# Reordering the first 45 microseconds of a fused attention and channel-mix kernel: the odd rows, mu, the norm products and the copy of v of block 1

## The chip, the cores and the metric

The kernel runs on one core of one Trainium2 chip. The metric is device time in microseconds (us) of that core. A kernel's time is the median of several executions, and most executions agree within 0.3%. The span that the trace shows is about 1.9 us shorter than the measured time of the same execution (510.4 against 512.35 us for the kernel before). All experiments ran beside executions of the kernel before on the same chip, and ratios are taken within such a call.

## The reference, cut to what matters

```python
# q, k, v: (4, 6208, 256) float32; x: (4, 6208, 256); d_ff = 1024
qn = q / (norm(q, axis=1) + 1e-6)             # column norms over all 6208 rows
kn = k / (norm(k, axis=1) + 1e-6)
s  = kn.transpose(0, 2, 1) @ qn / tau         # one 256 x 256 matrix per batch
a  = softmax(s, axis=-1)
x  = v @ a                                    # the attention's output

x_prev = x shifted by one row
xk = mu_k * x + (1 - mu_k) * x_prev           # xr the same with mu_r
out = sigmoid(xr @ w_r) * (relu(xk @ w_k) ** 2 @ w_v)
```

The first product with v needs the softmax of batch 0, and that needs *all* 6208 rows of q and k of batch 0. So nothing of the second half can start before 12.7 MB have been loaded. The work on batch 1 to 3 is then woven into the second half.

## The kernel before

The rows of q and k of batch 0 arrive in groups of 512, two smaller groups last. The 64 rows that are left over ("odd rows", group 0) are spread over a full tile that is cleared first. For every group VectorE (DVE) and ScalarE (ACT) cast to bf16 and square k, and TensorE (PE) adds to the covariances.

```python
def group_load(b, g):
    ...
            f = pq.tile([P, S, C], F32, ...)
            if g == 0:
                nc.vector.memset(f, 0.0)
                (nc.scalar, nc.gpsimd)[i].dma_start(f[0:P:P // (L // S)], qk_src(t, b, g))
            else:
                nc.sync.dma_start(f[:rows, :n], qk_src(t, b, g))
...
for g in order(0):                       # groups 1, 2, 0, 3, ... ; LAST is the last
    ...
    group_cast(g, pending)
    cov_first(g)                         # covariances of the group, on PE
    if g == DIRECT:                      # the last but two
        keep_warm(2)                     # two matmuls whose result nobody reads
        norms_first(DIRECT - 1)          # column sums of k squared, on PE
    if g > DIRECT:
        norms_first(g - 1)
    if g == NB - 1:
        v_load(0)
norms_first(LAST)
```

Then comes the chain from the last rows to the first block: the diagonals of q's covariance (DVE), two square roots (ACT), the table load for Exp (ACT), the scaling, four transposes (PE), Exp (ACT), the shares `a_sb` (DVE), the first products `x` (PE). PE takes its instructions in order. The loads of v and of the weights are issued from GpSimd (POOL) and cast to bf16 on the way. The v of blocks 0 to 3 is transposed on PE; from block 4 on a DMA transposes it.

```python
v_load(1)
nc.gpsimd.dma_start(w_k_sb, ...)
...
diagonals()
root(0)
root(1)
nc.scalar.activation(gate, ones[:, 0:1], AF.Exp)     # brings the table load forward
...
exp()
go = v_transpose_pe(1, nc.scalar.copy)   # 8 transposes on PE now; go() is the copy out, later
keep_warm(3)
weigh_first(0); weigh_first(1)           # a_sb
difference(1)
for a in range(2):
    for ih in range(2):
        product(a, ih)                   # the first x
    for dh in range(2):
        mix_first("xk", a, dh)
go()                                     # v of block 1 leaves PSUM here, on ACT
```

## Time and profile before

The kernel before takes 512.03 us (median of 3, 511.83 to 512.68). First the head of its page: the span, the busy time of each engine with its share of the span, and the busy tenths in 40 equal slices.

```profile
span 510.4 us, 9358 instructions
PE 484.9 (95%) x3450; PEld 331.0 (65%) x3450; DVE 447.1 (88%) x756; ACT 446.8 (88%) x927; POOL 101.7 (20%) x149
...
PE   3667999999999999999999999999999999999997
...
PEclk9999999999999999999999999999999999999999
```

PE is the full engine from the fifth slice on (one slice is 12.8 us), but for two waits of 1.2 us in all near 132 us. Its table of windows says the same with numbers. The first two figures of a line are the window and its length.

```profile
core 0: us, PE busy (x) PEld busy (x) DVE busy (x) ACT busy (x) POOL busy (x), PEclk, DMA share, GB/s
54.00:90.00 36.00, 35.88 (x257) 24.27 (x256) 33.47 (x52) 35.90 (x82) 11.00 (x19) 1.00 1.22 208
90.00:130.00 40.00, 40.00 (x294) 28.03 (x291) 39.27 (x59) 39.87 (x91) 10.69 (x16) 1.00 1.32 166
```

So a start of the stream one microsecond earlier is worth about one microsecond, and only the first 54 us can give it. The yardstick below is the first `vr` matmul, the first of the down-projection: from there PE is full. These are the lines of that head, from the timeline of the kernel before (start in us, duration, engine, line, operation, out<-in, count; in brackets the idle time just before it and what ended it):

```profile
start us, us, engine line op out<-in xcount [idle before <-releaser]
35.77 0.43 DVE L147 CAST qk<-f 128x512 bf16<-128x512 f32 x1
...
38.30 0.49 DVE L266 TENSOR_TENSOR dg<-s_ps,ident_f 128x128 f32<-128x128 f32 x2 [2.10 <-PE s_ps L183]
...
41.41 0.61 PE L359 MATMUL vT_ps<-ident,v_bf 128*128 128x128 bf16 x8
41.61 0.47 ACT L309 ACTIVATE e_sb<-st_ps,rn 128x256 f32<-128x256 f32 x1 [0.56 <-PE st_ps L301]
...
42.92 0.39 PE L404 MATMUL x_ps<-vT,a_sb 128*128 128x256 bf16 x2 [0.25 <-DVE a_sb L322]
...
45.22 1.03 ACT L365 COPY vT<-vT_ps 128x1024 bf16<-128x1024 bf16 x1
...
46.30 0.67 PE L428 MATMUL kT_ps<-xk,w_k_sb 128*128 128x256 bf16 x4 [0.66 <-ACT vT L365]
...
53.13 0.59 PE L380 MATMUL xT_ps<-vT,a_sb 128*128 128x512 bf16 x2 [0.22 <-DVE vT L365]
...
53.99 0.38 PE L521 MATMUL vr_ps<-w_r_sb,xr 128*128 128x256 bf16 x2
```

Read it so: the last rows of k land at 35.75 us, and their cast starts at 35.77; the diagonals (`dg`) start at 38.30, behind PE's covariances; Exp (`e_sb`) at 41.61. The first x product waits for the shares `a_sb`. The copy at 45.22 keeps PE waiting for 0.66 us. The first product of block 2 (L380) waits 0.22 us for its v.

### The profile page before, as it was taken

The page shows a single profiled execution, that of the slowest core. Times are in us where ns is not written, and L with a number is a line of the kernel's source. Part 1 is how long each engine was busy: PE and PEld are TensorE (multiplying, and loading weights), DVE is VectorE, ACT ScalarE, POOL GpSimd, SP SyncE. Part 2 cuts the span into 40 slices and gives each one's busy share as a digit, 9 for nine tenths or more (in the row PEclk, how much of TensorE's full clock was granted, in tenths as well). Part 3 has the DMA queues.
Part 4 walks back from the last instruction along what each step waited for, and adds up shares of the span by engine and source line. Part 5 has one row for each costly group of instructions (what it writes and reads, how often), then busy time and mean ns, then how long its engine had stood idle before and what let it go on. Part 6 is the DMA issues. An engine that isn't in the chain of part 4 may idle for free. (4 is left out here: it accounts for less than half of the span.)

```text
span 510.4 us, 9358 instructions
## 1 busy us (share of the span) xinstructions
PE 484.9 (95%) x3450; PEld 331.0 (65%) x3450; DVE 447.1 (88%) x756; ACT 446.8 (88%) x927; POOL 101.7 (20%) x149
## 2 busy tenths in 40 slices
PE   3667999999999999999999999999999999999997
PEld 1334666776566667667666677667666666666666
DVE  4867899999999999999979999999878787878884
ACT  4867999999899999999899999999897888878884
POOL 2044341223054132121243133000131100000000
PEclk9999999999999999999999999999999999999999
DMA  8999999999989999997599999924397653423123
GB/s 303 410 327 194 196 198 219 158 162 202 154 161 197 182 207 172 172 179 139 95 158 158 219 180 191 181 67 125 82 169 146 141 108 89 101 77 91 41 84 104
DMA packets 133423, 83.46 MB, mean 164 GB/s; under 512 B 50717, under 2 KB 126689, under 8 KB 133377
## 3 DMA queue, kind: packets, MB, share of 16 engines
q0 software_dynamic: 56688, 33.07, 50.1%
q1 hardware_dynamic: 76496, 49.59, 41.1%
q8 instruction: 27, 0.44, 0.4%
q10 hardware_dynamic: 192, 0.20, 0.1%
q14 instruction: 20, 0.16, 0.1%
HBM read 78.71 MB, written 25.43 MB: 204 GB/s over the span
## 5 line engine op out<-in xcount | busy, mean ns | idle before, releaser
L493 ACT ACTIVATE kr<-kT_ps 128x512 bf16<-128x512 f32 (+1 forms) x389 | 231.5, 607 | 28.0 <-PE kT_ps L488 24.1
L525 PE MATMUL vr_ps<-w_v_sb,kk 128*128 128x256 bf16 x1536 | 231.1, 273 | 0.2
L488 PE MATMUL kT_ps<-xk,w_k_sb 128*128 128x512 bf16 (+1 forms) x778 | 229.4, 377 | 0.1
L525 PEld LDWEIGHTS <-kk 128*128 128x128 bf16 x1536 | 149.5, 98 | 59.1 <-DVE kk L506 1.3
L535 DVE SCALAR_TENSOR_TENSOR res<-res,vr_ps 128x256 f32<-128x256 f32 x192 | 79.8, 416 | 42.6 <-ACT res L534 42.6
L506 DVE TENSOR_TENSOR kk<-kr 128x1536 bf16<-128x1536 bf16 (+2 forms) x148 | 116.9, 790 | 0.2 <-ACT kr L493 0.2
L488 PEld LDWEIGHTS <-w_k_sb 128*128 128x128 bf16 x778 | 75.3, 98 | 27.6 <-issue 0.6
L224 DVE TENSOR_TENSOR acc<-acc,sq 128x1024 f32<-128x1024 f32 x69 | 84.0, 1217 | 0.0
L534 ACT ACTIVATE res<-vr_ps 128x256 f32<-128x256 f32 x192 | 76.4, 398 | 1.3 <-PE vr_ps L525 1.3
L521 PE MATMUL vr_ps<-w_r_sb,xr 128*128 128x256 bf16 x384 | 73.3, 272 | 1.2 <-DVE res L535 1.2
L473 DVE SCALAR_TENSOR_TENSOR xk<-delta,mu_t,xT 128x512 bf16<-128x512 bf16 x94 | 70.0, 745 | 0.0
L473 DVE SCALAR_TENSOR_TENSOR xr<-delta,mu_t,xT 128x512 bf16<-128x512 bf16 x94 | 69.9, 744 | 0.0
L521 PEld LDWEIGHTS <-xr 128*128 128x128 bf16 x384 | 37.6, 98 | 46.4 <-issue 2.7
L382 ACT CAST xT<-xT_ps 128x512 bf16<-128x512 f32 x94 | 55.3, 588 | 12.2 <-PE xT_ps L380 12.1
L380 PE MATMUL xT_ps<-vT,a_sb 128*128 128x512 bf16 x188 | 55.9, 379 | 0.5 <-ACT xT L382 0.2
L236 PE MATMUL s_ps<-qk 128*128 128x256 bf16 (+1 forms) x294 | 55.8, 273 | 0.0
L130 POOL DMA_DIRECT2D qk<-in_q_dram x39 | 26.4, 676 | 143.1 <-ACT kr L493 61.1
L220 ACT ACTIVATE sq<-qk 128x1024 f32<-128x1024 bf16 (+1 forms) x49 | 51.0, 1040 | 0.0
L343 POOL DMA_DIRECT2D v_bf<-in_v_dram x48 | 36.8, 769 | 47.3 <-DMA vT<-v_bf 22.3
L183 PE MATMUL s_ps<-qk 128*128 128x384 bf16 (+1 forms) x104 | 20.2, 338 | 15.3 <-ACT qk L145 13.9
L463 DVE TENSOR_TENSOR delta<-xT 128x1024 bf16<-128x1024 bf16 x47 | 32.2, 686 | 1.8 <-ACT xT L382 1.8
L236 PEld LDWEIGHTS <-qk 128*128 128x128 bf16 (+1 forms) x294 | 28.5, 98 | 5.6 <-issue 0.8
(106 smaller groups left out, 249.2 us busy)
## 6 DMA issues: line engine op xcount, KB each, us to landing
out_dram<-res SPq DMA_DIRECT2D x47, 512.0 KB, 4.1
v_bf<-in_v_dram POOLq DMA_DIRECT2D x48, 256.0 KB, 9.2
qk<-in_q_dram POOLq DMA_DIRECT2D x36, 256.0 KB, 7.9
qk<-in_k_dram POOLq DMA_DIRECT2D x36, 256.0 KB, 8.8
f<-in_q_dram SPq DMA_DIRECT2D x11, 512.0 KB, 10.1
f<-in_k_dram SPq DMA_DIRECT2D x11, 512.0 KB, 10.2
vT<-v_bf SPq DMA_TRANSPOSE x44, 6.9
f<-in_q_dram SPq DMA_DIRECT2D x2, 256.0 KB, 9.0
```

Source lines behind the costliest of these rows:

```text
L224: nc.vector.tensor_tensor(sums[b], sums[b], t, op=OP.add)
L236: nc.tensor.matmul(s_ps[:, ih, :], rows_at(qk, b, g, 0)[:rows, s, ih * P:(ih + 1) * P], rows_at(qk, b, g, 1)[:rows, s, :], start=t0 and ih ...
L380: nc.tensor.matmul(xT_ps, a_sb[:, b, ih, dh * P:(dh + 1) * P], vT[:, :, ih, :], start=ih == 0, stop=ih == 1)
L382: nc.scalar.copy(xT[:, dh, 1:], xT_ps)
L473: nc.vector.scalar_tensor_tensor(o[:, dh], st[i, "d"][:, dh], mu[:, dh:dh + 1], st[i, "x"][:, dh, :M], op0=OP.mult, op1=OP.add)
L488: nc.tensor.matmul(kT_ps[:, :m], w_k_sb[:, dh, fh * P:(fh + 1) * P], xk[:, dh, :m], start=dh == 0, stop=dh == 1)
L493: nc.scalar.activation(kr, kT_ps[:, :m], AF.Relu, scale=0.5 ** 0.5)
L506: nc.vector.tensor_tensor(st[i, "kk"][:, fh // 4 * 4 + lo:fh + 1, :m], kr, kr, op=OP.mult)
L521: nc.tensor.matmul(vr_ps[:, D:], xr[:, dh, s * P:(s + 1) * P], w_r_sb[:, dh, :], start=dh == 0, stop=dh == 1)
L525: nc.tensor.matmul(vr_ps[:, :D], kk[:, fh, s * P:(s + 1) * P], w_v_sb[:, fh, :], start=fh == 0, stop=fh == 7)
L534: nc.scalar.activation(res[:, s], vr_ps[:, D:], AF.Tanh, scale=0.5)
L535: nc.vector.scalar_tensor_tensor(res[:, s], res[:, s], 1.0, vr_ps[:, :D], op0=OP.add, op1=OP.mult)
```

## The change

Its intent is to shorten that head. (1) The odd rows become one row per partition, 64 partitions, on ScalarE's queue ahead of everything, so that no tile has to be cleared and the work on them is small; mu is loaded last, behind the last group. (2) All norm products go behind the last covariances, two warming matmuls there go (and one of the three after the transposes of v of block 1), and the diagonals are issued between the last covariances. (3) The transpose and copies of mu move into the chain. (4) The copy of v of block 1 is made before x of block 0 instead of after it, and v of block 2 is transposed one slot later.

```diff
     def sizes(b):
-        return [S] * NB + [S // 2] * 2 if b == 0 else [1] + [S] * NB
+        return [1] + [S] * (NB - 1) + [S // 2] * 2 if b == 0 else [1] + [S] * NB
 ...
-                if g == 0:
-                    nc.vector.memset(f, 0.0)
-                    (nc.scalar, nc.gpsimd)[i].dma_start(f[0:P:P // (L // S)], qk_src(t, b, g))
-                else:
-                    nc.sync.dma_start(f[:rows, :n], qk_src(t, b, g))
+                (nc.sync if g else nc.scalar).dma_start(f[:rows, :n], qk_src(t, b, g))
 ...
     def cov_first(g, diagonal=None):
 ...                                   # after the last group's diagonal blocks:
+            diagonal()
 ...
-    nc.gpsimd.dma_start(mu_rows[0:2], moe_mu_k...)      # at the very start
-    nc.gpsimd.dma_start(mu_rows[2:4], moe_mu_r...)
 ...
+        if g == LAST:
+            nc.sync.dma_start(mu_rows[0:2], moe_mu_k...)
+            nc.sync.dma_start(mu_rows[2:4], moe_mu_r...)
         group_cast(g, pending)
 ...
-        cov_first(g)
-        if g == DIRECT:
-            keep_warm(2)
-            norms_first(DIRECT - 1)
-        if g > DIRECT:
-            norms_first(g - 1)
+        cov_first(g, diagonals)
 ...
-    norms_first(LAST)
+    norms_first()                      # all of them
 ...
-    diagonals()
     root(0)
     root(1)
 ...
+    mu_ps = ...; nc.tensor.transpose(mu_ps, mu_rows, ident_f[:4, :4])
     turn()
     invert_first(1)
     go()
+    nc.vector.tensor_copy(mu_t, mu_ps)
+    nc.vector.tensor_scalar_add(less, mu_t, -1.0)
     difference(0)
     exp()
-    go = v_transpose_pe(1, nc.scalar.copy)
-    keep_warm(3)
+    v_transpose_pe(1, nc.scalar.copy)()
+    keep_warm(2)
 ...
-    go()
 ...
-            if (i, j) in ((-1, 5), (0, 4)):
+            if (i, j) in ((-1, 6), (0, 4)):
                 v_transpose_pe(i + 3, nc.vector.tensor_copy)()
```

Left out: the sum of k's squares is split in two around k's cast, the copy of the second half of x is one instruction instead of two, and the third up-projection of block 0 is whole instead of in halves.

## The prediction

> **What bounds the kernel now.** From about 54 us on it is TensorE: the table of windows has PE busy 40.0 of 40 us in most stretches, and the trace shows two PE gaps over 60 ns after 54 us (0.82 and 0.35 us, near 132 us). So only the first 54 us count: when that stream starts.
>
> - Loads, 2 to 35.75 us. From 16 to 33 us the stream runs at its ceiling (about 410 GB/s, one 512 KB load per 1.28 us). 12.7 MB at that rate take 31.0 us; first packet 1.79 us, last landing 35.75 us (DMA issues and packets). About 2.5 us are lost early: 233 to 370 GB/s between 4 and 10 us, with single 4 KB packets of 0.9 to 1.6 us instead of 0.16. The Trainium skill ("DMA: Bandwidth & Descriptors", why a DMA increments by 16) says a DMA is done when all its engines are; here the rate falls from 34 us while the slowest finish.
> - Chain after the last load: DVE cast ends 36.20, but PE reaches the last cov group only at 37.55 (cov, two warming matmuls, norm products queue); the diagonal products start on DVE at 38.30, behind the last cov matmuls; Exp 41.61; first x product 42.92.
> - First block: ACT is full from 45 to 50 us, with the 1.03 us copy of v of block 1 (45.22) in front of kr; PE waits 0.66 us.
>
> **What changes, with costs**
> 1. Odd rows: the full-tile work of group 0 (casts 0.69+1.03, square 1.05, three adds 1.1 us, two 0.91 us memsets) shrinks to 64x256 pieces. ACT is behind only until 20 us, so by itself this is worth nothing. But no Pool-queue transfer (k rows, mu) runs inside the stream any more. If the stall at 4 to 6 us came from those, the stream ends earlier: I count 1.2 us (0 to 2.3).
> 2. Norms behind the last cov, warming matmuls out, second half of the k sums behind the k cast: PE starts the last group at 36.35 instead of 37.55. Diagonals are issued before the remaining four cov matmuls: DVE starts at 36.7 instead of 38.30. Those matmuls probably then wait for DVE's reads of the same banks, 0.3 us; norms (0.8 us in one run) finish by 38.5, the table load (1.28) by 40. Exp at 40.2 to 40.3: 1.4 us earlier.
> 3. mu copies move into DVE's chain (+0.35 us), which had nearly that slack: first x product about 1.3 us earlier.
> 4. v of block 1 copied in ACT's 1.18 us idle: xT of block 1 comes about 1.8 us earlier in all. But v of block 2 now goes behind a 0.6 us square on DVE, so the first product of block 2 (now 53.13) gains only 1.2 to 1.3.
>
> Sum: 1.25 (steps 2 to 4) + 1.2 (step 1) = 2.45 us, carried to the end by a saturated PE.
>
> **Predicted: 509.6 us, 80% range 507.7 to 511.2.** Faster by over 2%: 0.01; within 2%: 0.985; slower: 0.005.
>
> **What would show it.** Landing of the last k rows at about 34.5 (step 1); diagonals starting about 0.9 us after that landing, against 2.55 now (step 2); no ACT v copy between xT and kr (step 4); first vr matmul (now 53.99) at about 51.5.
>
> **What would make it wrong.** The early DMA stall has another cause and stays (about 510.8); 1 KB packets of the odd rows delay the head of the stream; PE turns cold without warming matmuls (the Trainium skill, "TensorE: Matmul & The Clock Gate", Part 1: idle windows halve the clock; here the first group takes 0.32 us per matmul, later ones 0.16); v or w landing late.

## More of the kernel before

The eight transposes of v of block 1 (L359) start at 41.41 and wait for nothing: that v had landed at 39.29, 2.1 us earlier.

The landing of v of block 0 and of block 1 is in the source view of the line that loads v, for the two issues at 33.3 and 34.1 us:

```profile
DMA to landing us min/median/max: 4.8/5.0/5.2
```

## The result, and the profile after

The changed kernel took 511.32 us (median of 4, 511.01 to 512.12) against 512.36 us for the kernel before (median of 4, 511.83 to 513.21). The ratio is 0.9981, with a 95% interval from 0.9962 to 0.9999. Here and below a ratio is the mean time of one kernel's fast runs over the mean of the other's in the same rounds, so it is not quite the ratio of the medians. That is within 2%, as predicted, but 1.7 us above the predicted time and above the range's upper end of 511.2.

From the page of the changed kernel:

```profile
span 510.2 us, 9336 instructions
...
PEclk9998999999999999999999999999999999999999
```

The fourth digit of the clock row is new: in the slice from 38 to 51 us PE did not have its full clock all the time. The timeline of the changed kernel shows what is there. The lines answer to those shown of the kernel before, with two more (L190 and L591).

```profile
34.84 0.43 DVE L149 CAST qk<-f 128x512 bf16<-128x512 f32 x1
...
35.49 0.49 DVE L272 TENSOR_TENSOR dg<-s_ps,ident_f 128x128 f32<-128x128 f32 x2 [0.23 <-PE s_ps L184]
35.84 0.69 PE L190 MATMUL s_ps<-qk 128*128 128x256 bf16 x4 [0.33 <-DVE dg L272]
...
39.11 0.46 ACT L315 ACTIVATE e_sb<-st_ps,rn 128x256 f32<-128x256 f32 x1
...
40.39 1.04 PE L365 MATMUL vT_ps<-ident,v_bf 128*128 128x128 bf16 x8 [1.50 <-DMA v_bf<-in_v_dram]
41.22 1.06 PE L591 MATMUL junk_ps<-fill,ones 128*128 128x512 bf16 x2
41.47 1.01 ACT L371 COPY vT<-vT_ps 128x1024 bf16<-128x1024 bf16 x1 [1.35 <-PE vT_ps L365]
42.08 0.63 PE L410 MATMUL x_ps<-vT,a_sb 128*128 128x256 bf16 x2
...
52.94 0.59 PE L386 MATMUL xT_ps<-vT,a_sb 128*128 128x512 bf16 x2 [0.83 <-DVE vT L371]
...
53.80 0.38 PE L527 MATMUL vr_ps<-w_r_sb,xr 128*128 128x256 bf16 x2
```

Everything up to Exp is where the prediction wanted it, or better: the last k rows land at 34.82 instead of 35.75, the diagonals start 0.67 us after that landing, Exp starts 2.5 us earlier. Then the line at 40.39 takes it back. The transposes of v of block 1 are now asked for at 38.89, but that v lands at 40.35. PE stands for 1.50 us, and the x products, which need none of it, are queued behind. The same eight transposes and the products then run slowly (1.04 us instead of 0.61, and 0.63 instead of 0.39 for two products): PE has half its clock, as the windows show.

```profile
core 0: us, PE busy (x) PEld busy (x) DVE busy (x) ACT busy (x) POOL busy (x), PEclk, DMA share, GB/s
36.00:38.00 2.00, 1.95 (x34) 1.74 (x32) 1.57 (x6) 0.67 (x3) 2.00 (x4) 1.00 1.06 107
...
40.00:42.00 2.00, 1.61 (x10) 1.14 (x11) 1.01 (x4) 0.65 (x3) 0.55 (x1) 0.50 1.12 209
42.00:44.00 2.00, 2.00 (x14) 1.53 (x13) 0.12 (x1) 1.01 (x3) 0.54 (x1) 0.71 1.16 203
```

The clock records put it at 0.5 from 39.76 to 43.18 us, 3.41 us long. And v of block 1, issued at 33.26 us, 0.8 us earlier than in the kernel before, took 7.1 us to land instead of 5.2 (source view of the line that loads v, for the same two issues; block 1 is the longer of the two):

```profile
DMA to landing us min/median/max: 5.1/6.1/7.1
```

Adding up the head of the two traces gives the balance. Each column is a difference of start or landing times from the trace.

| | last k rows land | landing to Exp | Exp to first x product | first x product to first vr | first vr |
|---|---|---|---|---|---|
| before | 35.75 | 5.86 | 1.31 | 11.07 | 53.99 |
| changed | 34.82 | 4.29 | 2.97 | 11.72 | 53.80 |
| gain | 0.93 | 1.57 | -1.66 | -0.65 | 0.19 |

The span follows that last column: it is first vr plus 456.45 us in both traces. What was won by Exp was lost before the first vr, and nothing after it.

### The profile page after: what moved, and what is told of

Its sections match the earlier page's. It is cut to its first block, busy times and chain, and to the rows that moved or that the text cites. A ratio compares the mean times of both kernels' runs of the same rounds, so it can differ in the third digit from the quotient of the medians.

```text
span 510.2 us, 9336 instructions
## 1 busy us (share of the span) xinstructions
PE 485.9 (95%) x3441; PEld 331.3 (65%) x3441; DVE 444.0 (87%) x751; ACT 446.3 (87%) x925; POOL 99.9 (20%) x146
## 5 line engine op out<-in xcount | busy, mean ns | idle before, releaser
L190 PE MATMUL s_ps<-qk 128*128 128x384 bf16 (+2 forms) x98 | 20.3, 352 | 16.0 <-ACT qk L147 14.9
```

## The experiments

There were 17 further runs. The theory was: the earlier chain asks for v of block 1 before it has landed, so PE, in order, waits in front of the x products, and the wait helps to halve its clock for 3.4 us. The rivals were that the earlier end of the loads, or the shorter chain, is not real but a draw of the traces; that the new place of the copy or of v of block 2 cost it; and that moving the odd rows and mu between the queues delayed v. The results first; the kernels of one call ran on the same chip.

| kernel | median (low to high), us | ratio to before, 95% |
|---|---|---|
| call 1, before 512.34 | | |
| v1_is_v0 (wrong) | 511.60 (510.02 to 519.03) | 0.9987 [0.9954, 1.0021] |
| warm_gap | 510.58 (509.97 to 513.05) | 0.9971 [0.9952, 0.9989] |
| v2_j5 | 510.99 (509.40 to 512.43) | 0.9971 [0.9949, 0.9993] |
| pool_head | 509.89 (509.32 to 510.79) | 0.9950 [0.9937, 0.9964] |
| call 2, before 511.79 | | |
| after_again | 511.77 (510.07 to 512.36) | 0.9989 [0.9970, 1.0008] |
| mu_pool | 510.77 (510.18 to 513.78) | 0.9982 [0.9957, 1.0006] |
| k_pool | 510.34 (509.75 to 511.69) | 0.9966 [0.9946, 0.9986] |
| head_j5 | 510.44 (509.44 to 514.40) | 0.9979 [0.9951, 1.0007] |
| call 3, before 511.86 | | |
| before_again (one look) | 512.17 | |
| before_vcopy | 512.26 (511.91 to 513.04) | 1.0005 [0.9991, 1.0019] |
| head_diag_late | 510.15 (509.51 to 511.11) | 0.9962 [0.9948, 0.9977] |
| head_warm_vt | 516.78 (515.37 to 526.96) | 1.0088 [1.0069, 1.0106] |
| call 4, before 512.99 | | |
| after_third | 510.83 (509.49 to 512.72) | 0.9962 [0.9944, 0.9980] |
| pool_head_again | 509.58 (509.41 to 510.58) | 0.9942 [0.9929, 0.9955] |
| pool_first | 510.14 (509.69 to 511.30) | 0.9954 [0.9941, 0.9967] |
| head_mid | 512.80 (510.68 to 515.24) | 1.0002 [0.9978, 1.0025] |
| call 5, before 512.78 | | |
| v1_behind_wk | 513.72 (513.45 to 514.95) | 1.0026 [1.0007, 1.0046] |

One run of v1_is_v0 and one of head_warm_vt were slow and are not in the ratios. The medians and ranges of the table do contain them: of the fast runs alone the medians are 511.13 us (v1_is_v0) and 516.36 us (head_warm_vt), the longest 515.8 and 518.01. All kernels but v1_is_v0 gave the right result.

### The changed kernel again, twice

No edit. Asked: is the late v a property of the change, or one bad draw?

> The changed kernel unaltered, for the spread. Its four runs so far took 511.0 to 512.1 us, all with a mean granted clock of 0.997, that is one half-clock window of 3.4 us each. If the wait for v of block 1 belongs to the kernel, most runs here show 0.997 to 0.998 and 511.0 to 512.1 us, and the trace shows v of block 1 landing after 39.5 us. If it was the chip or the draw, most runs show 1.0 and about 510 us.

> The changed kernel, as reference on this chip beside the next one. Expected from ten runs: spans of 509 to 510.5 us, no run with a mean clock of 1.0, v of block 1 landing 6.4 to 7.1 us after its issue, Exp to first vr 14.3 to 14.7 us.

after_again showed the same picture as the first trace: v of block 1 landed at 40.34, PE waited 0.72 us for it, the clock was 0.5 from 40.28 to 43.69, first vr at 54.04. after_third, on another chip, drew a better hand:

```profile
39.07 0.46 ACT L315 ACTIVATE e_sb<-st_ps,rn 128x256 f32<-128x256 f32 x1
39.16 0.62 PE L365 MATMUL vT_ps<-ident,v_bf 128*128 128x128 bf16 x8 [0.51 <-DMA v_bf<-in_v_dram]
39.62 0.38 PE L591 MATMUL junk_ps<-fill,ones 128*128 128x512 bf16 x1
...
40.26 0.39 PE L410 MATMUL x_ps<-vT,a_sb 128*128 128x256 bf16 x2 [0.27 <-DVE a_sb L328]
...
51.47 0.38 PE L527 MATMUL vr_ps<-w_r_sb,xr 128*128 128x256 bf16 x2
```

Exp starts at 39.07, practically where it did in the first trace (39.11). But v landed at 39.11, and a wait of 0.51 us for it costs nothing: the x product still waits for `a_sb`, as it did in the kernel before. The clock stays full, the first vr comes at 51.47, 2.5 us before that of the kernel before, and the span is 507.9 us. The same program thus has both outcomes, and the trace that the result came with was the bad one. The whole gain that was predicted exists in the good one.

How often each comes can be read from the mean clock of the runs that have no trace: one window of 3.41 us at half clock in 510 us makes a mean of 0.997. All 4 runs of the result had 0.997, and all 6 of after_again 0.997 or 0.999; of the 6 of after_third two had 1.0, and those took 509.78 and 509.49 us. A clock below 1.0 does not say where in the span the window fell (before_again, at 0.997, has it from 12.82 us on, and its first vr, at 53.94, is no later for it), so this is a count, not a place. A mean of 0.998 or 0.999 is less than one whole window; in the traces that have it (pool_head, pool_first, v2_j5, warm_gap) the clock was full in the head, and the half-clock stretch is cut off by the end of the span.

### v of block 0 in place of v of block 1

```diff
+    v0 = st[0, "v"]
     go = v_transpose_pe(0, nc.vector.tensor_copy)
 ...
     exp()
+    st[1, "v"] = v0
     v_transpose_pe(1, nc.scalar.copy)()
```

The result is wrong (relative error 0.19). It takes away what PE waits for, while the loads stay.

> The changed kernel, but the transposes for block 1 read v of block 0 (wrong result on purpose: the wait for v of block 1 is gone, everything else, its load too, stays). Theory: the change won 2.5 us up to Exp (41.61 to 39.11 us) and gave most of it back because PE, in order, waits 1.5 us for v of block 1 (landing 40.35) in front of the x products, and then runs at half clock for 3.4 us. So here: no PE gap before those transposes, first x product at 40.3 us (42.08 in the changed kernel, 42.92 before), no half-clock window, time about 1.4 us below the changed kernel (near 509.9). Rival: the later loads (w_k landing at 42.9, v of block 2) hold the start of the steady stream anyway: first x product early, but first vr matmul still at 53.8 and the time within 0.4 us of the changed kernel.

The wait at the transposes was gone and the first vr came at 52.69, 1.1 us earlier than in the changed kernel. The gain was not larger because the clock halved all the same, from 38.96 to 42.37 us, without any wait for v of block 1. The median of the fast runs, 511.13, is hardly below the changed kernel's. The traced execution is no example of it, as it took 515.8 us; there a later wait took the gain and more:

```profile
PE xT_ps L386 <- DMA vT<-v_bf: 2.4, 1, 2.4
```

(waits view of PE from 100 to 110 us: total, times, longest). From block 4 on v is transposed by a DMA. In the trace of before_again this v (block 7) landed at 101.5 us and was used at 104.4. Here PE asked at 103.9 and the transposed v came at 106.3, and the clock halved again after it. What the untraced runs (510.02 to 512.06 us when fast) waited for is not known. So the run is inconclusive as a time, and it taught two things: half clock needs no wait for v of block 1, and further down there are more loads with little slack. Waits of 0.3 to 2.4 us for transposed v near 102 to 116 us stand in the traces of several kernels with an earlier stream (this one, warm_gap, v2_j5, pool_head's first, head_mid), and in none of the kernel before or of the three of the changed kernel.

### Six warming matmuls in front of the transposes

```diff
     exp()
+    keep_warm(6)
     v_transpose_pe(1, nc.scalar.copy)()
```

> The changed kernel with six idle 512-column matmuls (1.3 us at full clock) between the transposes of S and those of v of block 1, where PE only waits. Theory: the half-clock window from 39.8 to 43.2 us costs PE about 1.3 us between 40.4 and 44.5; kept busy, PE keeps the full clock (granted 1.0 there), v transposes still start at about 40.4, first x product 41.3 instead of 42.08, last x product ends at 43.2 instead of 44.5, time 0.6 to 1.2 us below the changed kernel. Rival: the half clock costs nothing because the first block is bound by ScalarE and VectorE: same time within 0.3 us.

Median 510.58. PE's clock stayed full in the head, v had landed at 38.50 in this draw, and the x product started at 40.59, 1.77 us after Exp instead of 2.97 (the good draw of the changed kernel, above, has 1.19). The trace lost 2.11 and 1.03 us to the transposed v of later blocks, at 104 and 115 us. As v was in time in this trace, it does not tell what the matmuls alone did.

### The odd k rows and mu back on GpSimd's queue

```diff
-                (nc.sync if g else nc.scalar).dma_start(f[:rows, :n], ...)
+                (nc.sync if g else (nc.scalar, nc.gpsimd)[i]).dma_start(f[:rows, :n], ...)
 ...
     group_load(0, 0)
+    nc.gpsimd.dma_start(mu_rows[0:2], moe_mu_k...)
+    nc.gpsimd.dma_start(mu_rows[2:4], moe_mu_r...)
 ...
-        if g == LAST:
-            nc.sync.dma_start(mu_rows[0:2], ...); nc.sync.dma_start(mu_rows[2:4], ...)
```

pool_head has both parts, k_pool only the first, mu_pool only the rest. This undoes the part of the change that I had credited with the earlier end of the loads.

> The changed kernel with the odd k rows and both mu loads issued on GpSimd's queue at the head, as before the change; odd q rows stay on ScalarE's queue. Theory: transfers of GpSimd's queue inside the load stream cause the stall of 0.9 to 1.6 us packets at 4 to 6.5 us; it comes back here and the last k rows land at about 35.7 us (34.82 in the changed kernel, 35.75 before), everything behind 0.9 us later. Rival: the stall is chance or comes from the start of the stream itself: last landing 34.8 give or take 0.3, no packets over 0.9 us on several engines at once.

> The changed kernel with only the two mu loads back on GpSimd's queue at the head; odd k rows stay on ScalarE's queue. The kernel with both back on GpSimd's queue took 509.9 us at clock 1.0, against 511.3 at 0.997. Theory A: the mu loads, last on SyncE's queue, delay the v transfers that start at the same moment; then this one takes about 509.9 us at clock 1.0. Theory B: what counts is the place of the odd k rows (a first use of GpSimd's queue at the head); then this one stays at 511.3 us and 0.997. Theory C: it was the chip or the draw; then all kernels of this call lie within 0.5 us.

> The changed kernel with only the odd k rows back on GpSimd's queue at the head; mu stays last on SyncE's queue. Theory A (mu last delays v): about 511.3 us, clock 0.997. Theory B (a first use of GpSimd's queue at the head speeds its first v loads): about 509.9 us, clock 1.0. Theory C (draw): as the others of this call.

> Odd k rows and mu on GpSimd's queue at the head, again, on the same chip as the changed kernel. If it is truly better: 1 us or more below the changed kernel of this call, most runs at clock 1.0, v of block 1 landing 5.2 to 6.2 us after its issue, Exp to first vr 12.4 us. If the earlier call's chip made the difference: within 0.5 us of the changed kernel.

The last k rows landed at 34.79 and 34.92 in the two traces of pool_head, at 35.04 in k_pool and at 35.36 in mu_pool: early, with transfers on GpSimd's queue inside the stream. My cause for the earlier landing was wrong. And pool_head is the fastest kernel: 509.89 and 509.58 us on two chips, ratios 0.9950 and 0.9942. In both its traces v of block 1 landed at 39.01 and 39.10, in time, and first vr came at 51.58 and 51.69.

### One small transfer on GpSimd's queue at the start

```diff
     group_load(0, 0)
+    spare = const.tile([4, P], F32, name="spare")
+    nc.gpsimd.dma_start(spare[0:2], moe_mu_k...)       # 1 KB that nobody reads
```

Asked: does it help v of block 1 only that GpSimd's queue has been used early?

> The changed kernel with one 1 KB load into a spare tile on GpSimd's queue at the head and nothing else altered (mu still last on SyncE's queue, odd k rows still on ScalarE's). Theory B, a first use of GpSimd's queue at 33 us is slow to start: v of block 1 lands 5.2 to 6.2 us after its issue, time 1 us below the changed kernel of this call. Rival, the place of the mu loads or of the odd k rows matters by itself: landing 6.4 to 7.1 us after issue, time as the changed kernel.

510.14 us; v of block 1 landed at 39.25, in time, and first vr came at 51.53. The ratio, 0.9954, is better than those of the changed kernel in the two earlier calls, but in the same call after_third had 0.9962 and its interval covers this one. So it is not shown that the small transfer does anything.

### v of block 1 late on purpose

On top of pool_head, v of block 1 is issued behind the load of w_k instead of ahead of it. Nothing else moves.

```diff
-    v_load(1)
     nc.gpsimd.dma_start(w_k_sb, ...)
+    v_load(1)
     next_load()
```

> The kernel with odd k rows and mu on GpSimd's queue at the head (509.6 to 509.9 us, Exp to first vr 12.4 us), with the load of w_k issued in front of that of v of block 1. Theory: v of block 1 lands near 42.7 us instead of 39.1, PE waits about 3.6 us in front of the x products, the clock halves behind that wait, Exp to first vr rises by 3.5 to 5 us and the time by 3 to 4.5 us, to about 513 to 514 us. Rival: there is slack between the x products and the steady stream, and a late v of block 1 costs less than half of its delay.

```profile
42.41 1.03 PE L365 MATMUL vT_ps<-ident,v_bf 128*128 128x128 bf16 x8 [2.48 <-DMA v_bf<-in_v_dram]
...
44.09 0.63 PE L410 MATMUL x_ps<-vT,a_sb 128*128 128x256 bf16 x2 [0.22 <-issue]
```

v landed at 42.37 and PE waited 2.48 us; the clock halved from 41.64 to 45.06; the first x product came at 44.09 and the first vr at 55.75. The median is 513.72, in the range that was written down (513 to 514), and against pool_head's ratio of 0.9942 or 0.9950 it is now 1.0026. All six runs had a mean clock of 0.997 or below. This is the same failure as in the changed kernel, made by one moved line, and it makes the best kernel slower than the kernel before. The wait was expected to be 3.6 us and was shorter, because v landed 0.3 us sooner than expected and the chain was later here (Exp at 39.97). The run shows that a late v of block 1 is enough: landing 3.3 us later than in pool_head, it put off the first vr by about 4.1 us.

### Only the earlier copy, on the kernel before

```diff
-go = v_transpose_pe(1, nc.scalar.copy)
+v_transpose_pe(1, nc.scalar.copy)()
 ...
-go()
```

> The kernel before with one part of the change alone: ScalarE copies v of block 1 right behind Exp, ahead of x of block 0. Theory: the copy falls into 1.2 us of ScalarE's idle time, PE no longer waits 0.66 us for it at 46.3 us, xT of block 1 comes about 0.8 us earlier and, with v of block 2 still ahead of the square, the first product of block 2 gains 0.6 us or more: time 0.5 to 1.0 us less than before. Rival: VectorE (xk, xr, the copy of v of block 2) bounds the first block: gain under 0.3 us.

512.26 us, ratio 1.0005: nothing. PE's 0.66 us wait at 46.30 is gone from the trace. But a halved clock from 40.78 to 44.19 slowed the x products of this trace (first x at 43.02, x to vr 10.94), and v of block 2 then sets the next product. Two of the timed runs had the full clock and still took 512.22 and 513.04 us, so it is not the clock alone that hides the gain.

### v of block 2 one slot earlier

```diff
-            if (i, j) in ((-1, 6), (0, 4)):
+            if (i, j) in ((-1, 5), (0, 4)):
```

v2_j5 is this on the changed kernel, head_j5 on pool_head.

> The changed kernel with v of block 2 transposed and evacuated one slot earlier, as before the change (ahead of the square of kr 4 and 5 on DVE, not behind it). Theory: the PE wait of 0.83 us in front of the first product of block 2 (at 52.94 us) shrinks to about 0.2 and the time falls by 0.5 us. Rival: v of block 2 or the kT buffers then hold PE elsewhere (transposes at about 49.2 waiting, or up products waiting for the buffer), and the time is the same or worse.

> Odd k rows and mu on GpSimd's queue at the head, and v of block 2 transposed one slot earlier, as before the change. If both gains add: PE waits about 0.2 us instead of 0.83 before the first product of block 2, 509.4 us or less. Rival: the DMA transposes of v of blocks 7 to 9 are late for the earlier stream (waits of 1 to 3 us near 102 to 116 us in four of the traces), so a still earlier stream only waits longer there, and the time stays at 509.9.

This is the first product of block 2, in v2_j5 and then in pool_head, which keeps the later slot:

```profile
50.31 0.59 PE L386 MATMUL xT_ps<-vT,a_sb 128*128 128x512 bf16 x2 [0.23 <-DVE vT L371]
```

```profile
50.72 0.59 PE L386 MATMUL xT_ps<-vT,a_sb 128*128 128x512 bf16 x2 [0.83 <-DVE vT L371]
```

The later slot costs 0.6 us: the interval from first x product to first vr is 10.61 us in v2_j5 and head_j5 and 11.21 in pool_head and after_third. The prediction had this cost in its sum. But in time nothing came of taking it away: head_j5 has 510.44 (0.9979) where k_pool of the same call has 510.34. v2_j5's trace lost 0.34 and 0.43 us to transposed v of later blocks; head_j5's trace is the shortest of all (507.67 us), but some of its runs took up to 514.4. What those runs waited for was not traced.

### The diagonals issued late again

On pool_head, `diagonals()` back to its old place behind all the last covariances.

```diff
-            diagonal()                 # between the last covariances
 ...
     difference, product = x_first()
+    diagonals()
     root(0)
```

> The kernel with odd k rows and mu on GpSimd's queue at the head (509.9 us in an earlier call) with the diagonals issued behind the norm products, as before the change. Prediction's step 2: diagonals start behind the last cov matmuls, 0.5 to 0.8 us later after the last landing (0.75 us there); those matmuls no longer wait 0.33 us for DVE. Exp and the first x product come 0.4 to 0.8 us later, the time rises by as much. Rival: Exp waits for the table load behind the second root, that is for the norm products, and not for the diagonals: Exp as early or earlier, time the same.

510.15 us, where pool_head has 509.89. The time doesn't settle it: the ratio, 0.9962, is 0.6 to 1.0 us worse than pool_head's 0.9950 and 0.9942, which is the size of the loss that was feared, but across calls, and the intervals overlap. ACT's timeline does show that Exp came no later after the last landing. First pool_head, then head_diag_late:

```profile
37.59 0.17 ACT L276 ACTIVATE rn<-bank 128x2 f32<-128x2 f32 x1 [0.84 <-PE bank L204]
37.78 1.28 ACT L664 ACT_TABLE_LOAD   x1
...
39.19 0.46 ACT L315 ACTIVATE e_sb<-st_ps,rn 128x256 f32<-128x256 f32 x1
```

```profile
37.37 0.15 ACT L275 ACTIVATE rn<-bank 128x2 f32<-128x2 f32 x1
37.55 1.28 ACT L664 ACT_TABLE_LOAD   x1
...
39.35 0.47 ACT L314 ACTIVATE e_sb<-st_ps,rn 128x256 f32<-128x256 f32 x1 [0.31 <-PE st_ps L306]
```

With early diagonals the first root is early, but the second root waits 0.84 us for the norm products on PE (`bank`), the table load waits behind it, and Exp behind that. Landing to Exp is 4.40 us with the early diagonals and 4.22 with the late ones, where Exp waits for the score transposes instead (before: 5.86, and 5.57 in before_again). So in these traces the early diagonals gave nothing before Exp. That it is the emptier queue of PE that paid in step 2 is what is left over; no run put the norm products back alone.

This trace has v of block 1 in time (landed 39.27) and a halved clock from 39.58 to 42.99. Exp to first vr is 13.69 us in it and 12.39 in pool_head. The code after Exp is the same, so a halved clock in this place costs about 1.3 us by itself. v1_is_v0, with a halved clock and no wait either, has 13.48, or 1.1 us more than pool_head. The changed kernel's first trace has 14.69, 2.3 us more: about half of its loss is the clock, and the rest goes with the wait.

### The kernel before again

No edit, one look. Asked: does the DMA stall at 4 to 6 us, which I took for the cause of the late landing, always come?

> The kernel before, one more trace, for the spread of its load stream. The prediction read one trace: last k rows landing at 35.75 us, with a stall of ten packets at 4.6 to 6.6 us. Seven traces with the new head landed at 34.5 to 35.4 us, one of them (v of block 2 one slot earlier) with the same kind of stall. If the new head is worth about 0.9 us, this lands at 35.4 to 36.1; if the first trace was an unlucky draw, at 34.5 to 35.2. v of block 1 lands 5 to 6 us after its issue, so near 39.3.

The rows give the GB/s in slices of 1 us from the start, for the kernel before, for before_again, and for v2_j5, one fence each:

```profile
GB/s 0 33 332 414 311 233 356 344 348 370 406 406 426 401 406 406 426 401 406 410 422 401 406 414 418 401 406 414 418 406 401 397 393 377 214 138 184 185 139 176
```

```profile
GB/s 0 57 365 414 303 262 373 348 342 369 393 414 410 414 401 414 410 414 401 410 414 414 401 410 414 414 401 410 414 414 401 397 385 356 162 125 171 195 112 153
```

```profile
GB/s 0 49 307 397 354 202 386 389 401 422 414 422 422 406 434 406 406 406 422 406 406 406 422 406 401 410 422 406 406 406 422 381 387 360 122 155 158 142 154 185
```

All three dip at 5 to 6 us, and v2_j5, with the deepest dip (202) and a run of packets of about 1 us in it, landed its last rows at 34.77. before_again had hardly any such packets and landed at 35.99. What sets the kernel before apart in these rows is rather 7 to 10 us, where its two executions move 342 to 370 GB/s and the other 389 to 422. That is a description, not a cause; before_vcopy, with 381, 326 and 393 GB/s there, landed at 35.67.

### Two attempts at a still better kernel

head_warm_vt is head_j5 with four warming matmuls ahead of the transposes instead of two behind, and with the loads and DMA transposes of later v one block earlier, each with one buffer more. head_mid is head_j5 with the transposes of v of block 1 moved between the two halves of the x products, where they cannot stand in front of the first half, and five warming matmuls instead of two.

```diff
 # head_warm_vt                                    # head_mid
     exp()                                              exp()
+    keep_warm(4)                                  -    v_transpose_pe(1, nc.scalar.copy)()
     v_transpose_pe(1, nc.scalar.copy)()           -    keep_warm(2)
-    keep_warm(2)                                  +    keep_warm(5)
 ...                                                ...
-                v_load(i + 6)                          for a in range(2):
+                v_load(i + 7)                     +        if a:
 ...                                               +            v_transpose_pe(1, nc.scalar.copy)()
-                v_transpose(i + 5)                         for ih in range(2):
+                v_transpose(i + 6)                            product(a, ih)
```

> Meant to beat both: odd k rows and mu on GpSimd's queue at the head, v of block 2 one slot earlier, four idle matmuls ahead of the transposes of v of block 1 instead of two behind them, and v loads and DMA transposes issued one block (10 us) earlier with one more buffer each. Theory: the late DMA transposes of blocks 7 to 9 (waits of 0.3 to 2.4 us near 102 to 116 us in five traces) come from too late an issue into a full DMA queue; issued a block earlier they land in time. No PE wait there, no half-clock window at 40 us, median about 509.3 us and little spread. Rival: the DMA engines are simply full from 35 to 130 us, so transposes in front delay the q and k loads of batch 1 and PE waits for those instead: no better than 509.9.

> Odd k rows and mu on GpSimd's queue at the head, v of block 2 one slot earlier, and the transposes of v of block 1 between the two halves of the x products, with five idle matmuls in front of those products. Theory: x products start with the weights at about 40.3 us whatever v of block 1 does, and no half-clock window opens at 40 us; ScalarE's copy of v of block 1 then stands between the two halves of xT, about 0.6 to 0.9 us in the way. Exp to first vr 12.2 to 12.7 us in every draw; median 509.8 to 510.3 us, with less spread than the changed kernel. Rival: half-clock window opens all the same, or the copy costs more than 1 us: 510.5 or more.

Both missed. head_warm_vt took 516.78 us, slower than the kernel before (1.0088). Its head was early (first vr 51.87), but at 91.6 us PE waited 3.7 us for an output buffer (waits view of PE, 85 to 95 us), and the clock halved after it:

```profile
PE vr_ps L527 <- DVE res L541: 3.7, 1, 3.7
```

I take it that the output's stores, issued in order on SyncE behind transposes that were now asked for too early, came late; that was inferred and not tested. head_mid took 512.80 us (1.0002). In its trace the first x product needed no v of block 1 and came at 40.26, but the eight transposes still took their time on PE before the second half, PE waited 0.80 us for a `kr` of ACT at 43.90, and 0.40 and 1.48 us went to transposed v of later blocks. Moving the transposes away from one wait was not a gain.

## Why the prediction was wrong

**What bounds the kernel: right.** Before and after, the span is the first vr plus 456.4 to 456.5 us in the traces without later waits (before, changed, after_third). A start that is earlier by one microsecond is worth one, unless a later load is then missed.

**Step 1, the loads: size nearly right, cause wrong.** Predicted 1.2 us, measured 0.93 between the two traces. Over all traces, last landings were 35.67 to 35.99 with the old form of the odd rows (three traces) and 34.47 to 35.36 with the new one. But pool_head, k_pool and mu_pool have transfers on GpSimd's queue in the stream and land as early, and the stall is there with an early landing and missing with a late one. The Trainium skill ("DMA: Bandwidth & Descriptors", Issuing engines are not separate DMA queues) says that transfers share the same 16 DMA engines whoever starts them; these landings, as early with some transfers on GpSimd's queue as without, agree. That the size came out near is luck, since the cause was not the one given. Which part of the change brings it stays open: no run put the old layout of the odd rows back alone.

**Step 2, the chain to Exp: right in size, half right in cause.** Predicted 1.4 us; landing to Exp shrank by 1.57 us between the two traces, and by 0.9 to 1.6 over all pairs of a trace with the old chain (5.46 to 5.86) and one of the changed kernel (4.27 to 4.52). The 0.3 us wait of the last covariances for the diagonals came as predicted (0.33). But the early diagonals were not what brought Exp forward: head_diag_late has none, and its trace reaches Exp as soon after the landing (4.22 us).

**Step 3, the first x product about 1.3 us earlier: this is the step that failed.** It followed only the chain of Exp and DVE to the x product, which ends in the shares `a_sb`. Exp did come 2.5 us earlier, but the x product came only 0.84 us earlier. In front of it in PE's queue stand the transposes of v of block 1. In the trace before they had 2.1 us of slack (asked for at 41.41, v there since 39.29). The prediction moved the asking forward by more than that slack, to 38.89, and never set the two numbers side by side; "v or w landing late" stood only among the things that could go wrong, without a cost. In the changed kernel v then landed not at 39.3 but at 40.35. The term that the sum lacked is 1.66 us (Exp to first x, 1.31 to 2.97), and half clock took more after it.

**Step 4, xT of block 1 about 1.8 us earlier in all: fell with it.** PE's 0.66 us wait for ACT's copy did go, and the cost of v of block 2 behind a square (0.83 us of wait instead of 0.22) was in the sum. In a good draw the first x product to the first vr is 11.21 us against 11.07 before, so the two cancel. In the bad draw the halved clock made it 11.72.

**The sum.** Predicted 2.45 us: 1.2 for the loads and 1.25 for the rest. The traces of the result give 0.93 and -0.74, 0.19 in all. after_third, the same kernel, gives 0.95 and 1.57, 2.52 in all. The sum held in that execution, in which v is in time (though the cause of step 1 was wrong there too): it took 509.78 us against 509.6 predicted. One more run of the changed kernel had the full clock; it took 509.49 and has no trace.

The clocks of the timed runs tell how the average is made up, over all calls (fast runs; changed is the result's runs, after_again and after_third; pool_head both calls):

| mean clock of a run | before | changed | pool_head |
|---|---|---|---|
| 1.0 | 511.82 us (23 of 55) | 509.63 us (2 of 16) | 509.67 us (8 of 11) |
| 0.998 or 0.999 | 511.92 us (4 of 55) | 511.32 us (5 of 16) | 510.35 us (2 of 11) |
| 0.997 | 513.03 us (28 of 55) | 511.64 us (9 of 16) | 510.58 us (1 of 11) |

At full clock the changed kernel gains 2.2 us on the kernel before, near the predicted 2.45. But 9 of its 16 runs had a whole half-clock window, and 5 more, with less than a whole one, were hardly faster; none of these five was traced, so what they lost is not known, and the clock is not all of it. The kernel before draws such windows too, and its runs with one are 1.2 us longer. The table mixes chips and small numbers, and shows the direction rather than the digits.

**What stays open** is why v of block 1 lands late in the changed kernel more often than in pool_head. It took 7.1, 6.7 and 5.9 us from issue to landing in the three traces of the changed kernel, 5.9 and 5.8 in the two of pool_head, and 5.2 to 5.6 in the three traces with the old head. Over all traces that issue this load at its usual place, it took 5.5 to 7.1 us in the six new heads that use GpSimd's queue for nothing before the loads of v, and 5.2 to 6.4 in the nine that do use it: a tendency with overlap. In the two late traces of the changed kernel all DMA traffic between 36 and 38 us was slow: 107 GB/s in the changed kernel's window shown above and 109 in after_again, against the 161 of this window of after_third, and 147 in pool_head:

```profile
36.00:38.00 2.00, 2.00 (x36) 1.82 (x34) 1.59 (x6) 0.71 (x3) 2.00 (x3) 1.00 1.22 161
```

That goes with the late landing, but not always (head_warm_vt has 163 there and v at 40.01), and why the rate is low is not shown. k_pool and mu_pool, with half of pool_head's edit each, lie between the two within their intervals.

**What the clock records add.** This was counted from the traces, and no run tested it. In every trace with two half-clock records their starts are a multiple of 3.4133 us apart, to about a nanosecond (138 times in the changed kernel, 20 times between 38.96 and 107.22 us in v1_is_v0). So the windows lie on a fixed grid, and its phase differs from execution to execution. The last record of a trace gives its grid. Over 19 traces and about 2,760 such windows between 9 and 505 us, count the columns that PE's matmuls stream in a window (the second number of the shape: 1 for a norm product, 128 for a transpose, up to 512 for the others). The clock was half in the window after 13 of them, and these had 0 to 2,699 columns, one 2,831. No other window at full clock had fewer than 2,747.

In the changed kernel's window from 36.35 to 39.76 us there were 1,790 columns. Without the wait the eight transposes (1,024) and the first warming matmul (512) would have fitted in and made about 3,300, so by this count it was the wait that halved the clock there. In after_again it would have been about 2,600 to 2,800, at the edge. By this count, a phase of the grid that halves the clock in the head has a share of 44 to 47% in the two traces of the kernel before, 13 to 19% in those of pool_head and in after_third, and over half in the two late traces of the changed kernel. These are estimates; the timed runs had a whole window in 28 of 55, 1 of 11 and, over early and late v, 9 of 16.

**The best version** is pool_head: the change with the odd k rows and mu put back on GpSimd's queue at the start. It beats the kernel before by 0.50 and 0.58% in two calls, and was ahead of the changed kernel in the call that ran both (509.58 against 510.83; the intervals of the ratios overlap a little there, 0.9929 to 0.9955 and 0.9944 to 0.9980).

## What to carry to other kernels

When a change makes an engine reach its work earlier, list every load that this engine's queue waits for in that stretch, with its slack in the trace before, and compare each slack with the planned gain: the first one that is smaller can be the new bound, and an in-order queue passes it on to work that doesn't need the load. (It is harmless as long as that work has something else to wait for: 0.51 us in after_third cost nothing.) Look at more than one trace before you explain a difference of a microsecond; here the same kernel had a span of 510.2 in one and 507.9 in another, and the mean clock of untraced runs showed how often. And an earlier piece on one path to a join (here the diagonals) brought Exp no nearer while the other path (the norm products and the table load) ended later.

## What the Trainium skill lacked or had wrong

- "TensorE: Matmul & The Clock Gate", Part 1, gives a free-running window of 3413 ns and a rule of no idle gaps of PE over about 3.4 us. Length and free running agree: the half-clock windows quoted here are 3.41 us, on a grid whose phase differs by execution. But the rule is too lenient here: the clock halved for a window around a wait of 1.50 us (changed kernel), of 0.72 us (after_again), and with no wait for v of block 1 at all (v1_is_v0), while the kernel before had an idle gap of PE of 1.72 us ahead of its score transposes and kept its full clock. What went with a halved clock in these traces was not a gap's length but fewer than about 2,700 to 2,830 columns streamed in one window of the grid.
- "DMA: Bandwidth & Descriptors", Anatomy of one DMA, gives a fixed cost of about 2.0 us plus the bytes over 436 GB/s. It lacks what a transfer from GpSimd's queue takes in a stream of others: one and the same load of v (block 1, 256 KB) took 5.2 to 7.1 us from issue to landing in these traces, 8.1 behind the load of w_k, and varied by over 1 us between two executions of one kernel.
- "ScalarE: Activation LUTs", What ACT_TABLE_LOAD costs, has about 1283 ns for the load and a drain of about 1380 ns with it. The load agrees (1.28 us). The drain does not show here: in pool_head the table load starts at 37.78, 0.02 us after the root before it ends, and the next activation starts at 39.08, 0.02 us after the load ends.
